# A ScalarE exponential and a VectorE read of the same PSUM tile, declared independent

## The chip, the cores and the metric

The kernel runs on one core of a Trainium2 chip. The metric is the device time of one execution in microseconds (us), from launch to the end on that core. The engines are TensorE (PE in the profile, with its weight loads shown apart as PEld), VectorE (DVE), ScalarE (ACT), GpSimd (POOL) and SyncE (SP). Each engine works through its own list of instructions in order; an instruction waits on semaphores that other engines raise.

## The reference

`x` is a bfloat16 matrix of 2048 rows and 640 columns. Two branches read it, and a gate mixes them:

```
qkv = x @ wqkv                        # 32 heads of 20 columns each
p   = softmax(q k^T * 20**-0.5)       # 2048 x 2048 per head
a   = (p v, heads side by side) @ wo
h   = x @ w1 + b1                     # 640 -> 1536
b   = (h * tanh(softplus(h))) @ w2    # Mish, 1536 -> 640
g   = sigmoid(sum(x * gate_w))
out = g * a + (1 - g) * b
```

The softmax needs 32 x 2048 x 2048 = 134 million exponentials. They are by far the largest piece of elementwise work.

## The kernel before

**Groups and units.** Heads are taken four at a time: `p` counts eight quads of heads. Queries are taken 512 at a time: `qc` counts four chunks. A pair (p, qc) is a group `G`; there are 32 groups, worked through in order. Inside a group the keys come in 16 blocks of 128. A unit is one head `t` of the quad against one key block `j`: its scores are a tile of 128 keys by 512 queries in float32, which fills exactly one PSUM bank. No maximum is subtracted: a bound on the scores is worked out beside the main work, and a second, slower attention stands behind a branch at the end that is not taken with these inputs.

**Iterations.** The units are gathered into 819 iterations. Even iterations use the PSUM tile `S0` of three banks, odd ones `S1` of two (`WIDTHS = (3, 2)`). Each tile exists once, so TensorE can fill one while ScalarE reads the other. In an iteration `emit_qk` issues one matmul per bank (line 1092), and `emit_exp` issues one exponential over the banks together (line 1107), 1536 or 1024 columns wide, which writes the bfloat16 tile `E`. Later, `emit_set` multiplies four units of one key block with the values and adds them up in the PSUM tile `acc` (line 1157).

**The third bank.** ScalarE does not take all units. In each of groups 1 to 30 the last key block's four units are computed by VectorE. Such a unit is put into the third bank of an even iteration. That iteration has three matmuls, but the exponential covers only the first two banks (n = 2, 1024 columns). VectorE reads the third bank in `jv_read` (line 734), turning the scores into 16-bit integers in `E_dve`; seven more VectorE instructions per pair of units (`jv_steps`) build the exponential from these integers. There are 120 such reads, four per group. Their spacing in iterations is set by `JV_GAPS[1] = (4, 2, 4, 2)`, so the four stand close together near the start of each group.

**What sets the order.** The whole order is written out while the program is built; nothing is rearranged afterwards. A planner keeps a model clock for each engine in `T`. `emit_qk(i + 1)` comes ahead of `emit_exp(i)`. After them come the matmuls with the values that are due, and then `pump` fills TensorE's remaining time with pieces of the other matrix products (projections, Mish branch, output), and with matmuls on a constant tile `busy` (line 1032) whose results are not used. VectorE's side work is kept in a list `slow` and issued by `run_slow` when the model clock has room for it. The planner lets the refill of a score tile wait for the later of the exponential's end and the third bank's read:

```
S_free[tag] = T["act"] + NS_EXP_SEEN
if i in S_read:
    S_free[tag] = max(S_free[tag], S_read.pop(i))
```

Its clock for ScalarE takes the later of "scores are full" and "ScalarE is free" (`T["act"] = max(T["act"], S_full.pop(i)) + NS_EXP[n]`); the read of the third bank does not enter there.

**What the semaphores do.** They are derived from the tiles that the instructions touch. In the built program each of the 120 exponentials of an iteration with a third bank waits for VectorE's read of that bank, and the next fill of `S0`, two iterations later, waits for the exponential alone, since the read is over by then.

Of the kernel before, what the change touches and what calls it, by code (L numbers as in the profile page):

```python
# [150 lines left out]
def kernel(  # L151
# [12 lines left out]
    nc = tc.nc  # L164
# [150 lines left out]
    extra = []  # L315
    pos = 0
    taken_by, iters_start = {}, {}
    while pos < len(units):
        i = len(iters)
# [27 lines left out]
    def it_at(G, j=0):  # L347
        return it_of[unit_at[(G, j)]] if G < len(groups) else NI
# [31 lines left out]
    def vec(ns, dep=0.0):  # L380
        T["dve"] = max(T["dve"], dep) + ns
# [37 lines left out]
    def steps(start, parts, deadline, line=None):  # L419


        seq[0] += 1
        slow.append([deadline, seq[0], start, deque(parts), line])

    def run_slow(limit):

        while True:
            heads = {}
            for x in slow:
                heads.setdefault(x[4] or x[1], x)  # L430
            todo = [x for x in heads.values() if max(T["dve"], x[2]) + x[3][0][0] <= limit]
            if not todo:
                break
            x = min(todo, key=lambda x: x[:2])
            ns, fn = x[3].popleft()
            vec(ns, x[2])
            fn()
            if not x[3]:
                slow.remove(x)
# [278 lines left out]
    ROUND = 1.5 * 2.0**23  # L718
    jv_set = {}
    jv_at = {}  # L720
    jv_slot = {}
    halves = {}
    jv_emitted = set()

    def jv_read(G, k, t, slot, ps, full):

        if slot == 0:
            n = jv_set[(G, k)] = len(jv_set)
            assert n < 2 or n - 2 in jv_emitted, (G, k)
        n = jv_set[(G, k)]  # L730
        jv_slot[(G, k, t)] = slot
        run_slow(full + 100.0)
        vec(690, full)
        nc.vector.tensor_scalar(  # L734
            out=E_dve[n % 2].bitcast(I16)[:, slot, :], in0=ps, scalar1=ROUND,
            scalar2=ROUND - 512.0 * JV_BIAS, op0=ALU.add, op1=ALU.subtract,
        )
        if slot % 2 == 1:
            left = (it_at(G + 1) - now[0]) * 1115.0
            due = T["act"] + (min(left - 4000.0, 9000.0) if k < len(mine_of[G]) - 1 else left - 4000.0)  # L740
            steps(T["dve"], jv_steps(G, k, slot // 2), due, "exp")

    def jv_steps(G, k, half):
        V = nc.vector
        E, w, u = (
            t.rearrange("p a n -> p (a n)")
            for t in (E_dve[jv_set[(G, k)] % 2][:, 2 * half : 2 * half + 2, :], w_dve, u_dve)
        )
        e, wi = E.bitcast(I16), w.bitcast(I16)

        def mantissa():
            V.tensor_scalar(
                out=wi, in0=e, scalar1=511, scalar2=0x4000, op0=ALU.bitwise_and, op1=ALU.bitwise_or
            )

        def exponent():
            V.tensor_scalar(
                out=e, in0=e, scalar1=-512, scalar2=2, op0=ALU.bitwise_and, op1=ALU.logical_shift_right
            )

        def square():
            V.tensor_tensor(out=w, in0=w, in1=w, op=ALU.mult)  # L762

        def factor():
            V.tensor_scalar(out=u, in0=w, scalar1=EXP_A, scalar2=EXP_C, op0=ALU.add, op1=ALU.mult)

        def factor2():
            V.tensor_scalar(out=w, in0=w, scalar1=EXP_B, scalar2=None, op0=ALU.add)

        def product():  # L770
            V.tensor_tensor(out=w.bitcast(BF16), in0=w, in1=u, op=ALU.mult)  # L771

        def scale():
            V.tensor_tensor(out=e, in0=e, in1=wi, op=ALU.add)  # L774
            halves[(G, k)] = halves.get((G, k), 0) + 1
            if halves[(G, k)] == 2:
                jv_at[(G, k)] = T["dve"] + NS_SEEN

        return [
            (380, mantissa), (380, exponent), (640, square), (380, factor), (380, factor2),  # L780
            (640, product), (640, scale),
        ]
# [294 lines left out]
    def emit_qk(i):  # L1077
        a, n = iters[i]
        w = WIDTHS[i % len(WIDTHS)]
        tag = f"S{i % len(WIDTHS)}"  # L1080
        ps = spool.tile([P, w * QC], F32, tag=tag, name="Sp")
        S_of[i] = ps
        T["pe"] = max(T["pe"], S_free.get(tag, 0.0))
        S_full[i] = T["pe"] + NS_SCORES_SEEN
        worked(T["pe"], 215.0, 0.5)
        T["pe"] += NS_SCORES
        todo = [(units[a + k][0], units[a + k][1], units[a + k][3], units[a + k][4]) for k in range(n)]
        if extra[i] is not None:
            G, p, k, t, slot = extra[i]
            todo.append((G, p, mine_of[G][k], t))  # L1090
        for k, (G, p, j, t) in enumerate(todo):
            nc.tensor.matmul(  # L1092
                ps[:, k * QC : (k + 1) * QC],
                lhsT=kT[p][32 * t : 32 * t + 32, j * P : (j + 1) * P],
                rhs=qT[G][32 * t : 32 * t + 32, :],
                tile_position=(32 * t, 0),
            )
        if extra[i] is not None:
            G, p, k, t, slot = extra[i]
            jv_read(G, k, t, slot, ps[:, n * QC : (n + 1) * QC], S_full[i])  # L1100
            S_read[i] = T["dve"] + 60.0

    def emit_exp(i):
        a, n = iters[i]
        which = i % len(WIDTHS)
        E = ep[which].tile([P, WIDTHS[which] * QC], BF16, tag=f"E{which}", name="E")
        nc.scalar.activation(  # L1107
            E[:, 0 : n * QC], S_of.pop(i)[:, 0 : n * QC], ACT.Exp, scale=LN2 / 512.0
        )
        late[0] += max(0.0, S_full[i] - T["act"])  # L1110
        T["act"] = max(T["act"], S_full.pop(i)) + NS_EXP[n]
        tag = f"S{i % len(WIDTHS)}"
# [3 lines that stand above are left out]
        for k in range(n):  # L1116
            E_of[a + k] = E[:, k * QC : (k + 1) * QC]
            E_full[a + k] = T["act"] + NS_EXP_SEEN
# [175 lines left out]
    for i in range(NI):  # L1294
        now[0] = i
        if i + 1 < NI:
            emit_qk(i + 1)
        emit_exp(i)
        sets = emit_pv(iters[i][0])
        run_later(i)  # L1300
        while ready_h and ready_h[0][0] <= T["act"]:
            ready_h.popleft()[1]()
        run_slow(T["pe"] + QUEUE)
        pump(i, sets)
# [74 lines left out]
```

## Time and profile before

| | |
|---|---|
| three runs | 983.25, 989.17 and 991.75 us, median 989.17 |
| the profiled execution | 981.17 us, of which 979.4 us are the span from first to last instruction |
| granted TensorE clock, mean | 0.995 |
| ScalarE busy | 916.8 us, 94% of the span |
| TensorE busy | 874.1 us, 89% |
| VectorE busy | 744.3 us, 76% |
| exponentials of attention (line 1107) | 819, 896.4 us together |
| fills of the score tiles (line 1092) | 2048 matmuls, 326.4 us together |
| reads of a third bank (line 734) | 120, 82.9 us together, 0.691 us each |

Busy time is the union of an engine's instructions, so two that overlap count once. "Idle before" a group of instructions is the time in which the engine did nothing just ahead of one of them, and the arrow names what ended it. A matmul's end is modelled by the profiler, so a busy TensorE is not one at its peak.

### The profile page before, as it was taken

How to read it: one execution, taken by the hardware profiler on the slowest of the kernel's cores; microseconds unless marked ns; L12 is line 12 of the kernel's file. 1: busy time of each engine (PE TensorE's matmuls, PEld its weight loads, DVE VectorE, ACT ScalarE, POOL GpSimd, SP SyncE). 2: the span in 40 equal slices, each digit the busy share in tenths (PEclk: the TensorE clock that was granted, in tenths of full speed). 3: DMA queues.
4: the chain of work that ended last, by engine and by line, in shares of the span. 5: the costliest groups of instructions: out<-in, count | busy, mean ns of one | idle time of the engine just before them, and what ended most of it. 6: DMA issues, size and time to landing. Idle time of an engine off the chain costs nothing.

```text
span 979.4 us, 15290 instructions
## 1 busy us (share of the span) xinstructions
PE 874.1 (89%) x6184; PEld 311.6 (32%) x6184; DVE 744.3 (76%) x1398; ACT 916.8 (94%) x873; POOL 24.4 (2%) x39
## 2 busy tenths in 40 slices
PE   8989888989898888889888889888989889999996
PEld 4433322223333333223322223222223233333332
DVE  4468788888887887888877888878888786786633
ACT  6999999999999999999999999999999999999995
POOL 4000100000000000000100000000000000000000
PEclk9999999999999999999999999999999999999998
DMA  9000100000100010001011001010000000100101
GB/s 273 15 1 1 29 1 21 20 3 1 29 1 21 1 30 1 21 1 48 14 27 25 21 1 29 1 48 1 21 1 21 1 1 15 41 7 8 42 21 36
DMA packets 25635, 22.00 MB, mean 22 GB/s; under 512 B 10088, under 2 KB 24312, under 8 KB 25560
## 3 DMA queue, kind: packets, MB, share of 16 engines
q1 hardware_dynamic: 22808, 14.28, 5.4%
q0 software_dynamic: 1520, 5.94, 2.0%
q8 instruction: 49, 0.80, 0.3%
q10 hardware_dynamic: 1232, 0.76, 0.3%
q14 instruction: 26, 0.21, 0.1%
HBM read 15.73 MB, written 5.24 MB: 21 GB/s over the span
## 4 chain that ended last, share of the span: by engine, by line
ACT 55%; issue 17%; PE 16%; DVE 11%; DMA 1%; POOL 1%; POOLq 0%; ACTq 0%; DVEq 0%
ACT E L1107 52%; PE Sp L1092 8%; DVE E_dve L734 7%; ACT e L548 3%; PE acc L1157 2%; PE ps L490 2%; PE ps L638 1%; PE ps L607 1%; DMA wv<-in_A_wqkv_dram 1%; DVE h L618 1%; PE ps L518 0%; PE ps L683 0%; DVE ot L1329 0%; DVE T L1125 0%; DVE kT L505 0%
## 5 line engine op out<-in xcount | busy, mean ns | idle before, releaser
L1107 ACT ACTIVATE E<-Sp 128x1024 bf16<-128x1024 f32 (+1 forms) x819 | 896.4, 1220 | 44.1 <-DVE E_dve L734 40.8
L1092 PE MATMUL Sp<-qT,kT 32*128 32x512 bf16 x2048 | 326.4, 382 | 90.4 <-ACT E L1107 75.6
L1092 PEld LDWEIGHTS <-kT 32*128 32x128 bf16 x2048 | 115.5, 91 | 330.7 <-issue 307.9
L1157 PE MATMUL acc<-E,VA 128*21 128x512 bf16 x1928 | 191.3, 386 | 1.3 <-DVE T L1125 1.1
L734 DVE TENSOR_SCALAR E_dve<-Sp 128x512 int16<-128x512 f32 x120 | 82.9, 691 | 63.2 <-PE Sp L1092 62.2
L1032 PE MATMUL ps<-busy 128*128 128x512 bf16 x357 | 110.3, 384 | 0.0
L1157 PEld LDWEIGHTS <-VA 128*21 128x21 bf16 x1928 | 47.6, 88 | 109.1 <-issue 108.8
L607 PE MATMUL ps<-xT,w1t 128*128 128x512 bf16 x240 | 76.1, 388 | 0.0
L638 PE MATMUL ps<-w_sb,cell 128*128 128x320 bf16 x384 | 75.2, 303 | 0.0
L618 DVE TENSOR_SCALAR h<-ps,b1f 128x512 f32<-128x512 f32 x48 | 35.8, 747 | 22.0 <-PE ps L607 21.8
L490 PE MATMUL ps<-xT,wkp 128*128 128x512 bf16 x155 | 48.4, 384 | 1.7 <-DVE xT L456 0.8
L490 PE MATMUL ps<-xT,wqp 128*128 128x512 bf16 x155 | 49.5, 385 | 0.0
L683 PE MATMUL ps<-wo_sb,cell 128*128 128x320 bf16 x248 | 48.2, 302 | 0.0
L570 DVE RECIPROCAL r<-r 128x128 f32<-128x128 f32 x48 | 45.4, 947 | 0.6
L1125 DVE STREAM_TRANSPOSE T<-acc 128x512 f32<-128x512 f32 x32 | 22.9, 717 | 26.7 <-PE acc L1157 26.4
L771 DVE TENSOR_TENSOR w_dve<-w_dve,u_dve 128x1024 bf16<-128x1024 f16 x60 | 41.1, 686 | 0.9
L774 DVE TENSOR_TENSOR E_dve<-E_dve,w_dve 128x1024 int16<-128x1024 int16 x60 | 41.1, 685 | 0.9
L1032 PEld LDWEIGHTS <-busy 128*128 128x128 bf16 x357 | 26.9, 97 | 44.6 <-issue 35.1
L762 DVE TENSOR_TENSOR w_dve<-w_dve 128x1024 f16<-128x1024 f16 x60 | 41.0, 684 | 0.0
L638 PEld LDWEIGHTS <-cell 128*128 128x128 bf16 x384 | 29.3, 97 | 34.7 <-issue 28.2
L579 DVE TENSOR_TENSOR e<-e,r 128x512 f32<-128x512 f32 x48 | 33.2, 692 | 1.6
L588 DVE TENSOR_TENSOR cell<-h,e 128x512 bf16<-128x512 f32 x48 | 33.0, 687 | 1.1
(105 smaller groups left out, 653.1 us busy)
## 6 DMA issues: line engine op xcount, KB each, us to landing
w1t<-in_B_w_dram SPq DMA_DIRECT2D x14, 480.0 KB, 4.0
b_dram<-Bt SPq DMA_DIRECT2D x4, 640.0 KB, 3.2
out_dram<-ot SPq DMA_DIRECT2D x14, 160.0 KB, 1.8
xs<-in_A_x_dram POOLq DMA_DIRECT2D x3, 640.0 KB, 7.2
w_sb<-in_B_w_dram POOLq DMA_DIRECT2D x1, 1920.0 KB, 13.4
ws<-in_A_wqkv_dram SPq DMA_DIRECT2D x13, 100.0 KB, 4.1
w1t<-in_B_w_dram POOLq DMA_DIRECT2D x2, 480.0 KB, 9.4
wo_sb<-in_A_wo_dram SPq DMA_DIRECT2D x4, 200.0 KB
```

The source lines that it names most:

```text
L490: nc.tensor.matmul(box["ps"][:, :], lhsT=wpad[:, kt, :, :].rearrange("p h d -> p (h d)"), rhs=xT[:, kt, chunk * QC : (chunk + 1) * QC], st ...
L570: V.reciprocal(out=r[:, Q], in_=r[:, Q])
L607: nc.tensor.matmul(box["ps"][:, :], lhsT=w1t[4 * c + ft // 3][:, kt, (ft % 3) * P : (ft % 3 + 1) * P], rhs=xT[:, kt, c * QC : (c + 1) * QC ...
L618: nc.vector.tensor_scalar(out=h, in0=box["ps"][:, :], scalar1=b1f[:, ft : ft + 1], scalar2=None, op0=ALU.add)
L638: nc.tensor.matmul(box["ps"][:, :], lhsT=act[(ft, c)][:, u * P : (u + 1) * P], rhs=w2_sb[:, ft, half * HALF : (half + 1) * HALF], start=(f ...
L683: nc.tensor.matmul(box["ps"][:, :], lhsT=OT[(p, c)][:, u * P : (u + 1) * P], rhs=wo_sb[0][:, p, cols], start=(k == 0), stop=(k == len(ps_l ...
L734: nc.vector.tensor_scalar(out=E_dve[n % 2].bitcast(I16)[:, slot, :], in0=ps, scalar1=ROUND, scalar2=ROUND - 512.0 * JV_BIAS, op0=ALU.add, ...
L771: V.tensor_tensor(out=w.bitcast(BF16), in0=w, in1=u, op=ALU.mult)
L1032: nc.tensor.matmul(ps[:, 0:n], lhsT=busy[:, :], rhs=busy_row(n), start=True, stop=True)
L1092: nc.tensor.matmul(ps[:, k * QC : (k + 1) * QC], lhsT=kT[p][32 * t : 32 * t + 32, j * P : (j + 1) * P], rhs=qT[G][32 * t : 32 * t + 32, :] ...
L1107: nc.scalar.activation(E[:, 0 : n * QC], S_of.pop(i)[:, 0 : n * QC], ACT.Exp, scale=LN2 / 512.0)
L1157: nc.tensor.matmul(acc[32 * t : 32 * t + DH + 1, :], lhsT=VA[:, j, 4 * p + t, :] if VB is None else VB[:, 4 * p + t, :], rhs=moving(t), st ...
```

## The change

The read's instruction is kept in `S_reader`, and after the exponential of an iteration that has a third bank, the two are declared to have no dependency:

```
+    S_reader = [None]
...
-        nc.vector.tensor_scalar(
+        S_reader[0] = nc.vector.tensor_scalar(
             out=E_dve[n % 2].bitcast(I16)[:, slot, :], in0=ps, scalar1=ROUND,
...
-        nc.scalar.activation(
+        exp = nc.scalar.activation(
             E[:, 0 : n * QC], S_of.pop(i)[:, 0 : n * QC], ACT.Exp, scale=LN2 / 512.0
         )
+        if extra[i] is not None:
+            tc.declare_no_dep(exp.ins, S_reader[0].ins, reason="reads of different banks")
```

In the built program every engine has the same instructions in the same order as before. The waits differ in three places. In 120 exponentials the wait for VectorE is replaced by a wait for TensorE's second matmul of the tile. The first weight load of the 120 fills that come two iterations later now waits for VectorE's read (its matmul waits for the exponential, as before). Five exponentials of the Mish branch get a wait for VectorE's `h`, which the removed waits had implied.

## The prediction

> **What bounds the kernel now.** I read the page first: shares, chain, costliest groups.
>
> ```profile
> span 979.4 us, 15290 instructions
> ...
> PE 874.1 (89%) x6184; PEld 311.6 (32%) x6184; DVE 744.3 (76%) x1398; ACT 916.8 (94%) x873; POOL 24.4 (2%) x39
> ...
> ACT 55%; issue 17%; PE 16%; DVE 11%; DMA 1%; POOL 1%; POOLq 0%; ACTq 0%; DVEq 0%
> ...
> L1107 ACT ACTIVATE E<-Sp 128x1024 bf16<-128x1024 f32 (+1 forms) x819 | 896.4, 1220 | 44.1 <-DVE E_dve L734 40.8
> ...
> L734 DVE TENSOR_SCALAR E_dve<-Sp 128x512 int16<-128x512 f32 x120 | 82.9, 691 | 63.2 <-PE Sp L1092 62.2
> ```
>
> ScalarE is busy 94% of the span and holds the chain that ends last. Of the 44.1 us in which it stands ahead of an exponential, 40.8 end with VectorE's read of a third bank. That read in turn waits for scores. Next, who waits for whom:
>
> ```profile
> PE Sp L1092 <- ACT E L1107: 75.6, 227, 1.2
> DVE E_dve L734 <- PE Sp L1092: 62.2, 93, 1.5
> ACT E L1107 <- DVE E_dve L734: 40.8, 107, 1.5
> ```
>
> The three waits form a ring: scores are filled, VectorE reads one bank, ScalarE may start, and TensorE refills when ScalarE is through. Third, the order of time at two reads of group 14:
>
> ```profile
> 434.18 1.09 ACT L1107 ACTIVATE E<-Sp 128x1024 bf16<-128x1024 f32 x1
> ...
> 434.84 0.69 DVE L734 TENSOR_SCALAR E_dve<-Sp 128x512 int16<-128x512 f32 x1 [0.48 <-PE Sp L1092]
> ...
> 435.56 1.94 ACT L1107 ACTIVATE E<-Sp 128x1024 bf16<-128x1024 f32 x2 [0.30 <-DVE E_dve L734]
> ...
> 436.64 0.39 PE L1092 MATMUL Sp<-qT,kT 32*128 32x512 bf16 x3
> ...
> 437.08 0.69 DVE L734 TENSOR_SCALAR E_dve<-Sp 128x512 int16<-128x512 f32 x1 [0.49 <-PE Sp L1092]
> ...
> 437.80 3.28 ACT L1107 ACTIVATE E<-Sp 128x1024 bf16<-128x1024 f32 x3 [0.30 <-DVE E_dve L734]
> ...
> 438.88 0.39 PE L1092 MATMUL Sp<-qT,kT 32*128 32x512 bf16 x3 [0.61 <-ACT E L1107]
> ```
>
> One exponential ends at 434.18 + 1.09 = 435.27. The read begins at 434.84 as the scores arrive, so its own scores were there 0.43 us before ScalarE came free. The read ends at 435.53, and only then, at 435.56, does the next exponential start.
>
> **ScalarE's side.** Two exponentials in one piece take 1.94 us, and one that starts from a standstill takes 1.02 in the trace, so one in the flow costs 1.94 - 1.02 = 0.92 (0.916 is the median over the 409 exponentials of 1024 columns without a third bank, end to end). Here the step from end to end was 435.56 + 1.02 - 435.27 = 1.31, which is 0.39 too much. Added up over all 120 iterations, these steps take 165.9 us; 120 x 0.916 = 109.9; the excess is **56.0 us**. The waits alone give a close figure: 40.8 us idle, and 107 x (1.02 - 0.916) = 11.1 for starting afresh, together 52. No more than 56 can be had from ScalarE, and nothing else about its work changes.
>
> **Whether the scores are there.** Without the wait the exponential needs its own two banks. Over the 120, the fill ends at the median 0.47 us before the previous exponential does, at the tenth percentile 0.28 us. The odd iteration after it has 0.82 us at the median. So these fills do not stand in the way at once.
>
> **TensorE's side, what is late next.** ScalarE can only stay ahead if TensorE's refills come earlier too. I put one window around each group's four reads, from the end of the exponential ahead of the first to the end of the one after the last:
>
> ```profile
> core 0: us, PE busy (x) PEld busy (x) DVE busy (x) ACT busy (x) POOL busy (x), PEclk, DMA share, GB/s
> ...
> 435.27:446.82 11.55, 10.07 (x70) 3.28 (x68) 8.78 (x18) 10.49 (x12) 0.00 (x0) 1.00 0.16 43
> ...
> 913.37:925.39 12.02, 11.23 (x83) 4.49 (x84) 9.16 (x17) 10.02 (x12) 0.00 (x0) 1.00 0.04 14
> sum 346.61, PE 295.49 PEld 103.48 DVE 268.87 ACT 305.86 POOL 5.43; mean PE 9.85 PEld 3.45 DVE 8.96 ACT 10.20 POOL 0.18
> ```
>
> All 56.0 us of excess lie in these 346.6 us. TensorE is idle in them for 346.61 - 295.49 = 51.1, a little less than ScalarE wants to give up. Window by window it differs: in the first shown it is idle 1.48 us against 1.45 of excess, in the last 0.79 against 2.43. Taking the smaller of idle and excess in each of the 30 windows and adding up gives **47.4 us**. The idle time also lies in the right place: the 120 fills two iterations after a read stand 43.0 us in total before they start, like the 0.61 at 438.88. TensorE's list holds the same filler matmuls (line 1032, 110.3 us) whatever its idle time is.
>
> That is a middle. It is low because the scores come 0.47 us early: TensorE may fall that far behind in a window and catch up in the calmer 20 us that follow, up to the 56.0. It is high because no engine uses its last idle microsecond. I take 47.4, with 40 and 56 as its ends; 40 is the 43.0 with some 3 us lost.
>
> **The new wait.** The fill two iterations later now waits, in its first weight load, for VectorE's read. Behind that load in TensorE's list stand the fill, the products with the values, and the filler. The read ends at the median 0.26 us after the previous exponential, the new exponential at 0.92, and the fill needs both. In the run before, 118 of 120 reads end before 0.92. I cost it at nothing; ScalarE's exponential is the cover. If VectorE falls behind, the cover ends 0.65 us later, and after it comes the fill's own 0.47. VectorE's order stays, and it is idle 346.6 - 268.9 = 77.7 us in these windows, more than the 56 by which they shrink.
>
> The weight load itself is a second item: in the trace this load begins at the median 0.43 us after the read's end, and in one case of 120 before it. If each load had to move behind a wait and lay bare, it would cost 120 x 0.091 us (the mean of a weight load on line 1092) = 11 us; if none does, nothing. I take nothing, since 119 loads already come after.
> [...]
>
> **Reading side by side.** The exponential and the read will now read neighbouring banks of one tile at once, which the trace does not show. The nearest row is the read beside the previous exponential on the other tile (434.84 to 435.27 above): the 120 reads take 680 to 693 ns, whether they overlap or not. So I take nothing. The other end is that the two exclude each other wholly, which gives back the 56 us and no more. There is no reason for a gain.
> [...]
>
> The five Mish exponentials with an added wait want an `h` that VectorE had finished by then; nothing.
>
> **Sum.** The profiled execution took 981.2 us (span 979.4 and 1.8 around it), so it would take 981.2 - 47.4 = 933.8. It lies 8.0 under the median of the runs, 989.2, so I predict for the median 989.2 - 47.4 = **942 us**. With the ends of the saving, 933 to 949; the runs before spread from 6 below to 3 above their median.
>
> **Rivals.**
> *TensorE takes over (11 in 100).* Against the forecast speak the busiest windows: in the last one TensorE is at 93.4% and ScalarE stands all the same. If it can't be driven beyond that share anywhere, the 30 windows shrink only to 295.5 / 0.934 = 316.4, a saving of 30.2, and the median is 959. For it: the small steps between TensorE's instructions that the profile names "issue". Against it: most of TensorE's idle time ahead of fills is a plain wait for ScalarE.
> *The reads exclude each other, or another wait stands in the same place (4 in 100).* No change, 989. The constant 680 to 693 ns speak against it.
> *VectorE's read is late and TensorE stands (4 in 100).* The new wait blocks TensorE's whole list. It costs something once a read ends later than 0.92 + 0.47 = 1.39 us after the previous exponential, against 0.26 now. With three more VectorE instructions of 0.69 in front of each, it would end at 2.33, and 0.94 x 120 = 113 us would take the place of the 56: slower by 57, about 1046. VectorE's 77.7 us of idle time in the windows speak against it; for it, the one read that began 0.96 us after its scores.
>
> **How the numbers follow.** The forecast has 81 in 100. A difference of 1% is about what a measurement of this kernel can tell from none. The forecast and nearly all of the first rival are faster by more: 0.92 (0.81 + 0.11); the second rival is the same, 0.04; the third slower, 0.04. The range runs from 928 (the 933 of the full 56 us, and the spread below) to 961 (the first rival's 959 and some spread), which leaves out less than 2 in 10.
>
> **What would show it.** ScalarE's idle time before line 1107 falls from 44.1 to under 10 us, and the entry for VectorE's read leaves it; the mean of the 1024-column exponentials rises, as 120 more overlap their predecessor; ScalarE's share goes to 96 or 97%, TensorE's to 93 or 94% at unchanged busy time; TensorE's wait for ScalarE falls from 75.6 to some 30. A wait of TensorE for VectorE's read of more than 5 us, an exponential longer beside a read, or ScalarE standing for scores by more than 15 us would make the forecast wrong.

## The result and the profile after

The changed kernel takes 934.61 us in the median of four runs (934.44 to 948.24), the kernel before 988.81 (983.25 to 991.75). The ratio is 0.9492, with a 95% interval of 0.9398 to 0.9587. (Each ratio here is estimated over all runs of both kernels, without those more than 1.5% above the fastest of their kernel, so it is not exactly the quotient of the medians.) The two profiled executions are 981.17 and 934.48 us, 46.7 apart. A second set of six runs of the changed kernel, beside eleven of the kernel before on one chip, gave medians of 935.58 and 982.62, 47.0 apart, and a ratio of 0.9527 (0.9497 to 0.9557).

The page of the changed kernel (the exponential is now line 1108, the score matmul 1093, the read 735, the product with the values 1160):

```profile
span 932.7 us, 15290 instructions
...
PE 866.7 (93%) x6184; PEld 303.9 (33%) x6184; DVE 741.8 (80%) x1398; ACT 908.5 (97%) x873; POOL 24.4 (3%) x39
...
ACT 65%; issue 16%; PE 14%; DVE 3%; DMA 1%; POOL 1%; ACTq 0%; POOLq 0%
...
L1108 ACT ACTIVATE E<-Sp 128x1024 bf16<-128x1024 f32 (+1 forms) x819 | 890.3, 1268 | 6.6 <-PE Sp L1093 3.7
...
L735 DVE TENSOR_SCALAR E_dve<-Sp 128x512 int16<-128x512 f32 x120 | 82.8, 690 | 40.4 <-PE Sp L1093 39.5
```

ScalarE's standstill ahead of an exponential is 6.6 us in place of 44.1, and VectorE's read is no longer what ends it. VectorE went from 11% to 3% of the chain that ends last. The waits between the engines:

```profile
DVE E_dve L735 <- PE Sp L1093: 39.5, 85, 1.1
...
PE Sp L1093 <- ACT E L1108: 35.7, 136, 0.7
...
ACT E L1108 <- PE Sp L1093: 3.7, 9, 0.8
...
ACT E L1108 <- PE acc L1160: 2.0, 7, 0.5
...
PEld L1093 <- DVE E_dve L735: 1.2, 4, 0.5
```

TensorE's wait for ScalarE is 35.7 in place of 75.6. Of the 6.6 us in which ScalarE still stands ahead of an exponential, 5.7 end with TensorE (3.7 with scores, 2.0 with a product). The new wait, that of a weight load for VectorE's read, ends last 4 times in 120, for 1.2 us together. (Ahead of these loads the profile names other VectorE instructions 52 times, 14.9 us; there the read had been over for 0.29 us or more, so it was not the read that held them.) The same place as shown before, the reads of group 14, in order of time:

```profile
410.94 5.17 ACT L1108 ACTIVATE E<-Sp 128x1536 bf16<-128x1536 f32 x5
...
412.95 0.69 DVE L735 TENSOR_SCALAR E_dve<-Sp 128x512 int16<-128x512 f32 x1 [0.51 <-PE Sp L1093]
...
415.11 0.69 DVE L735 TENSOR_SCALAR E_dve<-Sp 128x512 int16<-128x512 f32 x1 [0.41 <-PE Sp L1093]
...
415.51 0.39 PE L1093 MATMUL Sp<-qT,kT 32*128 32x512 bf16 x2
...
415.83 0.40 PE L1160 MATMUL acc<-E,VA 128*21 128x512 bf16 x4
...
416.31 2.37 ACT L1108 ACTIVATE E<-Sp 128x1024 bf16<-128x1024 f32 x2 [0.20 <-PE acc L1160]
```

Five exponentials run in one piece past both reads, where before each read stopped them. At 416.11 comes the new kind of loss: TensorE is late, its product with the values ends late, and the next exponential, whose output tile that product still reads, stands for 0.20 us. The same windows as before, around the four reads of each group; shown are group 14, group 30 and the sum:

```profile
core 0: us, PE busy (x) PEld busy (x) DVE busy (x) ACT busy (x) POOL busy (x), PEclk, DMA share, GB/s
...
413.36:423.77 10.41, 9.91 (x70) 3.10 (x68) 8.72 (x18) 10.21 (x12) 0.00 (x0) 1.00 0.16 47
...
867.91:878.52 10.61, 10.61 (x81) 3.95 (x81) 9.03 (x17) 10.20 (x11) 0.00 (x0) 1.00 0.05 16
sum 300.82, PE 289.19 PEld 95.95 DVE 257.16 ACT 297.05 POOL 5.46; mean PE 9.64 PEld 3.20 DVE 8.57 ACT 9.90 POOL 0.18
```

The 30 windows shrank from 346.6 to 300.8 us, and TensorE's idle time in them from 51.1 to 11.6. In group 14 it is 0.50 in place of 1.48; in group 30 it has none left.

Where the time went, from the ends of all 819 exponentials. "Too long" is the step from end to end beyond 0.916 us (1024 columns) or 1.343 (1536), in us over the kernel; reads 1 to 4 are the four of a group, 30 each:

| kernel | iteration with read 1 | 2 | 3 | 4 | iterations after a read | the rest |
|---|---|---|---|---|---|---|
| before | 14.5 | 12.1 | 13.1 | 16.3 | 2.5 | 24.5 |
| after | 1.0 | 0.7 | 0.7 | 2.1 | 8.0 | 24.7 |

The reads' own iterations gave back 51.5 of 56.0 us. The iterations after them took 5.5 again. With 0.7 us less at the start and 0.1 at the end, that is the 46.7, within the rounding. Not all of the excess is standstill: an exponential of the Mish branch, 0.51 us of work, stands ahead of 6 of the 120 iterations with a read and of 5 of those after a read, before and after the change. That is 3.1 us of the 56.0 and of the 4.5 that are left, and 2.5 us of the column after it. So the time lost at the reads fell from 52.9 to 1.4 us, and the time lost after them rose from nothing to 5.5. (The rest is mostly the other 37 Mish exponentials, some 19 us.)

### The profile page after: what moved, and what is told of

Read it like the earlier page. It is cut to its first block, busy times and chain, and to the rows that moved or that the text cites. A ratio compares the mean times of both kernels' runs of the same rounds, so it can differ in the third digit from the quotient of the medians.

```text
span 932.7 us, 15290 instructions
## 1 busy us (share of the span) xinstructions
PE 866.7 (93%) x6184; PEld 303.9 (33%) x6184; DVE 741.8 (80%) x1398; ACT 908.5 (97%) x873; POOL 24.4 (3%) x39
## 4 chain that ended last, share of the span: by engine, by line
ACT 65%; issue 16%; PE 14%; DVE 3%; DMA 1%; POOL 1%; ACTq 0%; POOLq 0%
ACT E L1108 62%; PE Sp L1093 5%; ACT e L548 3%; PE acc L1160 3%; PE ps L638 2%; PE ps L490 2%; DMA wv<-in_A_wqkv_dram 1%; PE ps L683 1%; PE ps L607 1%; PE ps L1033 1%; PE ps L518 1%; DVE ot L1332 0%; DVE h L618 0%; POOL xs L273 0%; DVE T L1128 0%
## 5 line engine op out<-in xcount | busy, mean ns | idle before, releaser
L1093 PE MATMUL Sp<-qT,kT 32*128 32x512 bf16 x2048 | 326.1, 382 | 51.3 <-ACT E L1108 35.7
L1093 PEld LDWEIGHTS <-kT 32*128 32x128 bf16 x2048 | 108.6, 91 | 292.5 <-issue 253.8
L638 PEld LDWEIGHTS <-cell 128*128 128x128 bf16 x384 | 29.3, 97 | 34.5 <-issue 28.0
L548 ACT ACTIVATE e<-h 128x512 f32<-128x512 f32 x48 | 34.9, 727 | 0.1
```

Of the source, the lines that this page charges most:

```text
L548: nc.scalar.activation(e[:, :], h[:, :], ACT.Exp)
L638: nc.tensor.matmul(box["ps"][:, :], lhsT=act[(ft, c)][:, u * P : (u + 1) * P], rhs=w2_sb[:, ft, half * HALF : (half + 1) * HALF], start=(f ...
L1093: nc.tensor.matmul(ps[:, k * QC : (k + 1) * QC], lhsT=kT[p][32 * t : 32 * t + 32, j * P : (j + 1) * P], rhs=qT[G][32 * t : 32 * t + 32, :] ...
```

## The experiments

### Half of the waits removed

Does each freed exponential save a fixed amount, or does TensorE's slack cap the sum?

```
         if extra[i] is not None:
+        (slots_0_2:  and extra[i][4] % 2 == 0)
+        (slots_1_3:  and extra[i][4] % 2 == 1)
             tc.declare_no_dep(...)
```

Reads 1 and 3 of each group freed:

> Only the first and third of each group's four exponentials are declared independent; the other 60 still wait for VectorE. In the kernel before, the steps of these 60 iterations are 27.6 us too long, those of the other 60 28.4 us. Theory A (TensorE's slack around the reads caps the gain, so half the gain meets half the squeeze): nearly all of the 27.6 comes back, 26 to 27.6 us, span 952 to 953.5. Theory B (each freed exponential loses a fixed piece, because it now runs beside the read or because of the new wait, some 0.08 us each): half of the 46.7 us that the whole change saved, 23 us, span 956.

Measured: 959.81 us median (959.25 to 960.41), ratio 0.9752 (0.9708 to 0.9795), span 958.5: 20.9 us saved. Both theories miss. Reads 2 and 4 freed:

> The other half: the second and fourth of each group's four exponentials are declared independent. Theory A: 27 to 28.4 us of the 28.4, span 951 to 952.5, and the savings of the two halves add up to 53 to 56 us, more than the 46.7 of the whole change. Theory B: some 24 us, span 955, and the halves add up to the 46.7 of the whole.

Measured: 960.62 (957.69 to 963.16), ratio 0.9768 (0.9716 to 0.982), span 956.4: 23.0 us saved. The halves add up to 43.9, which is less than the whole, not more. By place:

| kernel | read 1 | 2 | 3 | 4 | after a read | the rest |
|---|---|---|---|---|---|---|
| before | 14.5 | 12.1 | 13.1 | 16.3 | 2.5 | 24.5 |
| 1 and 3 freed | 1.0 | 15.0 | 0.5 | 18.7 | 2.9 | 23.6 |
| 2 and 4 freed | 14.4 | 0.5 | 13.4 | 2.1 | 5.5 | 24.3 |

The freed iterations gave back 26.1 and 25.8 us; Theory A said 26 to 27.6 and 27 to 28.4. What it had not foreseen is in the other columns: with 2 and 4 freed, the iterations after a read cost 3.0 us more than before; with 1 and 3 freed, reads 2 and 4 cost 2.9 and 2.4 us more. Their fills start 0.148 and 0.117 us after the exponential that frees the tile, in the mean, in place of 0.055: 30 x 0.093 and 30 x 0.062 are 2.8 and 1.9 us. So TensorE does come later. Where an exponential still waits for the read, each microsecond of that lands on ScalarE, since scores, read and exponential stand in a row; where it does not wait, the scores were 0.47 us early and the lag vanishes in that. That speaks for TensorE's lag and against a fixed price per read, but it was my reading after the fact, not what I had expected, and by the spans alone Theory B came nearer in both runs. The idle time that remains in the profile with 1 and 3 freed:

```profile
ACT E L1108 <- DVE E_dve L735: 24.8, 53, 0.9
```

### A shorter read, with the wait and without

VectorE reads 64 of the 512 columns; what these two kernels leave out is the rest of that part of the attention.

```
-            out=E_dve[n % 2].bitcast(I16)[:, slot, :], in0=ps, scalar1=ROUND,
+            out=E_dve[n % 2].bitcast(I16)[:, slot, 0:64], in0=ps[:, 0:64], scalar1=ROUND,
...
+    at(5, lambda: nc.vector.memset(E_dve[0], 0.0))
+    at(7, lambda: nc.vector.memset(E_dve[1], 0.0))
```

In the kernel before:

> The kernel before with VectorE's read cut to 64 of its 512 columns (the other columns of E_dve are zeroed once and then keep old numbers, so this part of the attention is left out), by the row of 0.691 us for 512 columns some 0.45 us shorter. Theory A (ScalarE's stall is the time from the scores' arrival to the read's end, less 0.47 us that ScalarE is busy anyway): a read that ends 0.45 us earlier ends before ScalarE comes free, the stall goes nearly whole, and the span falls to about the 933 of the changed kernel, 930 to 940. Theory C (the stall is a price of the wait itself, not of the read's length): it stays above 965.

Measured: 938.45 us median (937.71 to 946.69), ratio 0.9564 (0.9503 to 0.9624), span 935.9. Inside the range of Theory A, far from C. ScalarE's group of exponentials:

```profile
L1107 ACT ACTIVATE E<-Sp 128x1024 bf16<-128x1024 f32 (+1 forms) x819 | 890.5, 1226 | 8.4 <-DVE E_dve L734 3.9
```

The wait is there as before, and costs 3.9 us in place of 40.8. So the stall was the length of the read beyond the scores' early arrival, and nothing else about the wait. In the changed kernel:

> The changed kernel with the same shortened read (the same part of the attention left out). Theory A (nothing on the path waits for the read any more: it ends 0.6 us before the exponential that shares its tile): span 930 to 934, less than 3 us faster, though VectorE has 54 us less to do. Theory B (the new wait of TensorE, or the read beside the exponential, costs several us): 925 to 929.

Measured: 935.68 (934.88 to 945.0), ratio 0.9539 (0.9475 to 0.9604), span 933.1, against 932.7 with the whole read. The iterations after a read are still 7.3 us too long (8.0). So the read's length is off the path, though the reads are 56 us shorter in all, 0.47 each: the 5.5 us that come back are hardly due to it.

### The fourth read twice

```
-        nc.vector.tensor_scalar(
+        for _ in range(2 if slot == 3 else 1):
+            nc.vector.tensor_scalar(
```

In the kernel before:

> The kernel before, with the fourth read of each group issued twice on VectorE (30 more instructions of 0.69 us; the second writes the same numbers). Theory A: each exponential waits for the second read as well, 30 x 0.69 = 20.7 us, and a calm stretch of 20 us follows in which nothing can take that back; span 998 to 1001.

Measured: 1019.05, 1030.19 and 1032.33 us, and 1041.23 in a fourth run that the ratio leaves out; ratio 1.0469 (1.0396 to 1.0541). The lowest span is 1017.2, 16 us and more above the expectation: the direction is right, the size is not. The mean granted clock was 0.947 to 0.967 in the three runs (0.933 in the fourth), against 0.984 to 0.997 for the kernel before beside them. With 6.6 us for each 0.01 (the section on the hardware), the best run's distance from 0.995 is worth an estimated 18.5 us, which would leave a span of 998.7. That the rest is the clock is argued from this slope, which is drawn from clocks of 0.983 and more, and not shown by a run. The one trace kept, that of the fourth run, fits it: against the kernel before, the iterations with the fourth reads are 24.3 us longer, near the 20.7 of Theory A, and the rest, which the experiment does not touch, is 34.5 us longer. In the changed kernel:

> The changed kernel with the same doubled read; both reads are declared independent of the exponential. Theory A (the exponential, 0.92 us long, and then the 0.4 us by which scores come early, cover a read that ends up to 1.39 us after the previous exponential; the second read ends at about 0.31 + 0.69 = 1.00): span 932.5 to 935, less than 2 us. Rival (the new wait holds TensorE as soon as the read outlasts the exponential): the second read outlasts it by 0.1 us and more, 30 times, with TensorE's whole list behind it: 3 to 12 us, span 936 to 945.

Measured: 936.31, 936.92, 943.14 and 946.92 us, ratio 0.9581 (0.9519 to 0.9642). The first two, at clocks of 0.996 and 0.997, have spans of 934.5 and 935.1, at the upper edge of Theory A's range; the other two are 6 to 11 us longer, at clocks of 0.987 and 0.983. So 20.7 us of added reading cost about 2 where the exponential covers them. The rival is visible all the same, in the waits of the run with 0.987:

```profile
PEld L1095 <- DVE E_dve L737: 11.2, 27, 0.8
...
PE Sp L1095 <- DVE E_dve L737: 2.7, 9, 0.5
```

With the read ending 1.18 us after the previous exponential in place of 0.45, the new wait does hold weight loads 27 times. The matmuls behind them stand for 2.7 us only. The new wait is cheap because it is covered, and the cover is nearly used up at this length.

### A plan that knows of the wait

```
-        T["act"] = max(T["act"], S_full.pop(i)) + NS_EXP[n]
+        T["act"] = max(T["act"], S_full.pop(i), S_read.get(i, 0.0)) + NS_EXP[n]
```

> The kernel before, but the planner's clock for ScalarE now waits for the third bank's read, as the real instruction does, so that TensorE's pieces and 490 filler matmuls in place of 357 are laid out for the longer iterations. Theory A (the stall itself is what costs; the order of the rest is no matter): span 975 to 985. Rival D (the change gains because the chip then follows the plan, and a plan that fits would gain as well): 930 to 960.

Measured: 984.49 us median of ten (983.7 to 986.19), against 980.65, ratio 1.0036 (1.0018 to 1.0054), span 982.7. Theory A holds, rival D falls: the stalls are there as before (15.1, 14.4, 12.6 and 16.6 us at reads 1 to 4). The gain is the wait's, not the plan's.

### Attempts to win back the 5.5 us

Three kernels give TensorE more room around the reads. Reads farther apart:

```
-    JV_GAPS = {1: (4, 2, 4, 2), ...
+    JV_GAPS = {1: (4, 4, 4, 4), ...
```

> The changed kernel with the four reads of a group spread over it (distances of 4, 4, 4, 4 iterations or more in place of 4, 2, 4, 2), so that TensorE's three-bank fills do not follow each other as closely. Theory A (TensorE's lack of slack around the reads costs the 5.5 us that the iterations after a read lose): 2 to 5 us come back, span 928 to 931. Theory B (a fixed price per read): no change, 932 to 934. It can lose if the later reads delay the product that needs them at the group's end.

Measured: 944.82 us (944.36 to 945.79), ratio 0.9628 (0.9598 to 0.9657): slower than the changed kernel by some 10. It does not test the theory, because one standstill elsewhere eats everything. The granted clock by windows around it:

```profile
155.00:160.00 5.00, 3.39 (x18) 1.03 (x17) 4.17 (x9) 4.99 (x5) 0.00 (x0) 1.00 0.04 14
160.00:165.00 5.00, 0.39 (x2) 0.09 (x2) 4.76 (x9) 0.00 (x0) 0.00 (x0) 0.82 0.00 0
165.00:170.00 5.00, 3.16 (x19) 0.63 (x19) 3.21 (x6) 1.49 (x2) 0.00 (x0) 0.50 0.00 0
```

With the last read so late in the group, VectorE finishes the group's `E_dve` only at the group's end: TensorE's product with it waits 1.82 us. Behind it in VectorE's list nine instructions of the Mish branch stand ahead of the transpose that empties `acc`, and TensorE (first busy number) waits 5.7 us for that one. ScalarE (fourth) waits 8.5 us for scores, and from 163.2 us on, inside TensorE's standstill, its clock is granted at half rate. The last sentence of the expectation named this kind of loss; its price came as a surprise. Where the standstill does not reach, the sign is as Theory A says: after the fourth reads 2.6 us are lost in place of 4.4.

No filler matmuls in the iterations with a read and right after:

```
+            elif extra[i] is not None or (i > 0 and extra[i - 1] is not None):
+                break
             elif ch is None or ch.bank is not None:
                 cost = busy_matmul(ch)
```

> The changed kernel without filler matmuls on the constant tile in the iterations with a read and those right after them; 321 fillers are left of 357. Theory A (TensorE is short of time there): 1 to 4 us faster, span 929 to 932. Theory B (a fixed price per read): no change. If the granted clock falls for want of activity, it is slower.

Measured: 945.19 us (937.35 to 948.12), ratio 0.9582 (0.9524 to 0.964), span of the best 935.5. The iterations after a read are 6.6 us too long (8.0), those with a read 4.0 (4.5), the rest 28.9 (24.7). What is gained at the reads is lost outside, and the clock is 0.978 to 0.992.

One piece of side work less ahead of a read and at it:

```
+        if extra[i] is not None or extra[min(i + 1, NI - 1)] is not None:
+            limit -= 215.0
```

> The changed kernel with TensorE's side work laid out so that in the iteration ahead of a read and in the iteration with it one piece less (215 ns of the planner's clock) fits; 329 filler matmuls are left of 357. Theory A (the iterations after a read lose time because TensorE comes late to their scores): their 8.0 us too much fall to 3 to 5, span 928 to 931 at a clock of 0.996. Theory B (a fixed price of the exponential beside the read): no change. If the work comes back in one place, or the clock falls, it is slower.

Measured: 942.2 us (936.05 to 944.76), ratio 0.9586 (0.9548 to 0.9624), clocks 0.982 to 0.994. Theory A's 3 to 5 us are missed: the iterations after a read are 9.8 us too long in place of 8.0, and the rest 27.5 in place of 24.7. After the fourth read, where the most was lost, the loss did fall, from 4.4 to 3.0 us; after the first it rose from 0.9 to 3.7, where TensorE stood once for the emptying of `acc`, and half clock followed (0.73 in the mean from 130 to 135 us, 0.50 from 135 to 140):

```profile
PE acc L1162 <- DVE T L1130: 3.0, 1, 3.0
```

So none of the three beats the changed kernel. That TensorE's lateness causes the 5.5 us rests on the trace (the product at 415.83 above, the scores of the iteration after the fourth read) and on the lag in the half-way kernels. How much of it could be won back stays open.

### No filler at all

```
-    FLOOR = 0.54
+    FLOOR = 0.0
```

> The changed kernel without any filler matmul (357 fewer, 110 us of TensorE's busy time), and pieces of the side products only when they are due. Theory A: TensorE's slack around the reads grows, 3 to 6 us faster, span 927 to 930, as long as the granted clock stays at 0.99. If the fillers hold the clock, the clock falls below 0.97 and the kernel is slower than 945.

Measured: 1075.38 us (1071.89 to 1077.59), ratio 1.0913 (1.0861 to 1.0965), mean clock 0.75. The page's slices:

```profile
PEclk9999755555589986867999566555556658999998
```

TensorE has 110 us less to do and runs at half clock for long stretches. The second half of the expectation holds: the fillers, with the pieces of side products that the same line lets run ahead of time, buy the clock: in the four runs without them it is 0.742 to 0.752, in the first four of the changed kernel 0.977 to 0.996. Which of the two buys how much was not separated.

### The changed kernel once more

> The changed kernel once more, beside the kernel before on one chip, for the granted clock of each run. In 27 runs of the kernel before, the time goes from 978.8 us at a mean granted clock of 0.997 to 989.5 at 0.983, 6.6 us for each 0.01. Theory E (a standstill of TensorE behind ScalarE's stalls costs a whole clock window at half rate now and then; without the stalls it happens less often): most runs of the changed kernel at 0.995 or more, 933 to 936 us, where of the kernel before 9 of 27 are. Rival: the two kernels lose clock equally often, and the larger difference of the medians, 54 us against 46.7 in the two profiles, was chance.

Measured: 935.58 us (934.05 to 938.64), the kernel before 982.62 (979.23 to 988.05). Five of the six runs have a clock of 0.995 or 0.996, as Theory E has it; of the eleven of the kernel before beside them, five reach 0.995. With the first set, 8 of 10 runs of the changed kernel do, and 14 of all 38 runs of the kernel before whose clock is known; but these come from four chips, on which 1 of 7, 7 of 13, 1 of 7 and 5 of 11 reach it. And the medians lie 47.0 us apart here, so the 54 of the first set did not come again, which is what the rival says. Theory E stays open.

## Why the prediction was right, and where it was off

- **ScalarE's excess of 56.0 us** was the right term, 3.1 us too large: that much of it was the six Mish exponentials, which no change of a wait can remove. Of the other 52.9 us, 51.5 went. A shorter read took most of it away too, with the wait in place, so it was the read's length beyond the scores' early arrival.
- **TensorE as what is late next** was right, and the sum of the smaller of idle and excess, 47.4, came close to the 46.7 measured. The closeness of the sum was partly luck. Window by window the rule is off by 0.21 us in the mean, where a window shrank by 1.53: in the 11 windows where TensorE's idle time is smaller by more than 0.05 us it gives 15.3 us and 16.1 came, in the other 19 it gives 32.2 and 29.8 came. And the lag does not show at the reads, where 1.4 us of lost time remain, but in the iterations after them (5.5 us, from nothing). The step "these fills do not stand in the way at once" looked at the reads' neighbours only in the old timing, where they had 0.82 us to spare; after the change the median there is 0.42.
- **The fourth read's iteration** is the one I should have singled out. Its fill takes 0.59 us in the median, not 0.39 as for the first three. In all 30 of these fills two of the three matmuls use the same head and so the same `tile_position`; in the other 380 fills of three matmuls all positions differ, and they take 0.39 in the median. That the position is the cause is inferred from these medians; no run isolates it. 4.4 of the 8.0 us stand after it.
- **The new wait at nothing**: right. It ended last 4 times, for 1.2 us. The doubled read shows where the cover ends.
- **The weight load at nothing**: right. The 120 fills behind such a load stand 4.6 us in total before they start, in place of 43.0. So no run here shows the loss of up to 11 us that the prediction weighs. One reading there was wrong: in the kernel before, the load begins at the median 0.70 us after the read's end, and the 0.43 given there is about the tenth percentile, 0.42. That 119 of 120 come after it is right, and nothing else was worked out from it.
- **Reading side by side at nothing**: right. Exponential and read of one tile now overlap for 65.5 us in all; the reads take 678 to 693 ns (680 to 693 before), and the step of an exponential of 1024 columns is 0.917 us in the median, with a read or without.
- **The three rivals** fell: TensorE did go beyond the 93.4% of the busiest window (100% in the last one); nothing excluded anything; VectorE's reads began 0.07 us after their scores in the median, 0.04 before.
- **The predicted median, 942, was 7.4 us too high**, and the mis-sized term is the transfer to the median. I put the 8.0 us between the profiled run and the median of the runs before on top, as if they were scatter that stays. They did not stay: the changed kernel's median lies 0.1 us from its profiled run. Neither were they a fixed property of the kernel before, whose eleven runs in the second set have a median of 982.62; there the medians are 47.0 apart. In the runs whose clock is known the scatter goes with the granted clock; that the change removes part of it is not shown. At nearly equal clock (0.997 before, 0.996 after) the lowest runs are 979 and 934, 45 us apart, so some 2 of the 46.7 us go with the lower clock of the profiled run before, 0.995.

## What to carry to other kernels

When an engine that is busy 94% of the time waits for another engine's read of the same tile, ask whether the read and its own work touch the same bank. Here they did not: the wait cost the length of the read beyond the scores' early arrival, 52.9 us over 120 reads, and without it 51.5 of them went, while the reads stayed at 0.68 to 0.69 us and the step of 1024 columns at 0.916 and 0.917. Work out what the wait had been hiding, window by window, from the idle time of the engine that feeds both: here TensorE came late and took back 5.5 of the 51.5 us won at the reads. And where the run times scatter, look at the granted clock of each run before carrying a saving from one profile over to a median.

## What was not expected of the hardware

Much of the scatter goes with the granted TensorE clock. Over 27 runs of the kernel before, on three chips, the time goes from 978.8 us at 0.997 to 989.5 at 0.983; a straight line through them has 6.6 us for each 0.01. The profiles of the kernel before and of the changed one both end with a stretch at half rate after the last exponentials, 6.3 and 6.6 us, which takes 0.003 and 0.004 off the mean; no run here has a mean above 0.997. The profile of the kernel before holds one dip ahead of that, from 686.33 to 689.75 us; windows of its length, 3.41 us, around it:

```profile
679.50:682.92 3.42, 3.22 (x23) 1.01 (x22) 2.53 (x6) 3.06 (x4) 0.00 (x0) 1.00 0.00 0
682.92:686.33 3.41, 2.49 (x18) 0.83 (x15) 2.21 (x5) 2.92 (x4) 0.00 (x0) 1.00 0.03 5
686.33:689.75 3.42, 3.42 (x17) 0.72 (x14) 2.54 (x5) 2.65 (x3) 0.00 (x0) 0.50 0.19 11
689.75:693.16 3.41, 3.27 (x27) 1.39 (x24) 2.94 (x6) 3.41 (x5) 0.00 (x0) 1.00 0.39 133
```

In the second, TensorE was busy for 2.49 of 3.41 us, with two standstills of 0.44 and 0.47 us in which it waited for exponentials that had themselves waited for a read. The whole third is at half rate, with TensorE busy throughout, and the fourth at full rate again. The half rate lasted 3.41 us here; in the kernel with the reads farther apart it lasted four times as long, 13.65 us, beginning inside a standstill of TensorE of 5.7 us. What Theory E calls a clock window is such a stretch of 3.41 us.

The dip came after gaps of no more than 0.47 us, with TensorE busy 73% of the window ahead of it, so the full rate was lost without any longer gap. The busy share of the profile does not decide it either: counted in steps of 3.41 us from the dip, nine other windows ahead of the last exponential's end were less busy, 64 to 73%, with gaps of up to 1.24 us, and the full rate stayed after each. What decides is open.

So a stall on ScalarE may cost TensorE its clock, since at the reads TensorE waits too (the profile of the kernel before has the one dip above). That the change makes these dips rarer fits the 8 of 10 against 14 of 38 at 0.995 or more, but no run isolates it, and the kernel whose plan knows of the wait has all the stalls, with 490 filler matmuls in place of 357, and reaches 0.995 in 7 of 10 runs.
